# Linear attention beside routed tokens: which of the first transfers ScalarE issues first, and where the router's vector takes its turn

## The chip, the cores and the metric

The kernel runs on one core of one Trainium2 chip. The metric is the device time of one execution in microseconds. The kernel is one program for five engines that run side by side: TensorE (PE, matrix products and transposes; its weight loads are shown apart as PEld), VectorE (DVE), ScalarE (ACT), GpSimd (POOL) and SyncE (SP), which only issues transfers. SyncE and ScalarE each have a queue of transfers between HBM and the on-chip memory; in the profile SyncE's is q1 and ScalarE's is q10. An engine works through its own instructions in program order and waits for others by semaphores.

## The reference

One input x (2048 tokens of 640, bf16) is normalised per token, and two blocks are added to it:

```python
x = A_x
xn = _layernorm(x, axis=-1)
return x + _A_ref(xn, A_wqkv, A_wo) + _B_ref(xn, B_w_r, B_w_gate, B_w_up, B_w_down)
```

`_A_ref` is linear attention with 32 heads of 20: `qkv = xn @ wqkv`; `phi(t) = where(t > 0, t + 1, exp(t)) + 1e-6` on q and k; `kv = pk^T v` and `z = sum of pk` per head; the result is `(pq @ kv) / (pq . z + 1e-6)`, times `wo`.

`_B_ref` scores each token, `r = xn @ w_r`, takes the 8 tokens with the highest score, sends them through a gated layer (`silu(x w_gate) * (x w_up)`, times `w_down`), scales with `sigmoid(r)` and adds them back in their places; all tokens of xn are passed on too.

What matters here: `w_r` is a vector of 640 numbers, used once, for the scores. The k part of `wqkv` is 640 x 640. Both multiply the normalised tokens, so that both need the tokens turned (features on the partitions).

## The kernel before

The 2048 tokens are 16 tiles of 128 (`T = 16`), each with 640 features, which are 5 blocks of 128 (`KC = 5`). The program is one straight list written out by hand; no planner reorders it, so the order of the calls in the source is the order on each engine.

For each tile: its 160 KB of x are loaded by SyncE's queue into `x_sb`; VectorE takes statistics of the two halves (`ln_stats`, lines 165 and 168, then 169); the inverse root of the variance comes from ScalarE for tiles 0 and 1 (`root="A"`, lines 178 and 179, a logarithm and an exponential) and from GpSimd for later ones (lines 171 and 174); VectorE scales (`ln_scale`, line 183) into `xn`. Tiles 0 to 4 are turned by TensorE (`turn_pe`, line 195), and the turned blocks are copied from PSUM to `xnT` (`turned`, lines 203 and 205); later tiles are turned by a transfer. TensorE then makes k (`k_one` and `k_mm`, line 213), ScalarE and VectorE form phi(k) (`k_act`, `k_phi`), and TensorE gathers `xn^T phi(k)` (`g_mm`, line 274). From tile 4 on a loop interleaves k of one tile, a unit of q (`q_mm`, line 247) and the gathering of the tile before. Then come the routing, the small products per head, the eight chosen tokens, and the output loop (`o_mm`, line 789; `o_add`, line 799).

The first part, around the change:

- SyncE issues x tiles 0, 1 and 2 (lines 125, 127, 129), each 160 KB, then tile 3 (line 151) after a small GpSimd instruction. Tiles 4 and up are issued behind a GpSimd copy of tile 0's inverse root (line 303).
- ScalarE issues `wr_rows`, the vector w_r as 5 rows of 128, 1.2 KB (line 126), then the k weights in two pieces: feature blocks 0 to 2, 480 KB (line 128), and 3 to 4, 320 KB (line 130). Then it loads its table of functions.
- TensorE runs filler matmuls on a zeroed tile (`warm`, line 294) until there is work. Between the seventh and the eighth filler it turns w_r's rows into a column for each feature block (line 299) in PSUM bank 2; ScalarE copies them to `wrT` (line 310) ahead of its copy of the turned tile 0.
- `wrT` is used twice: as the last column of the k weights (`wk_sb[:, :, D]`, line 324), so that the scores of tiles 1 and up come with k, and by itself for tile 0 (line 331).
- Tile 0's k has its first six matmuls (feature blocks 0 to 2, lines 320 to 322) ahead of the turn of tile 1, its last four behind it.

Of the kernel before, what the change touches and what calls it, by code (L numbers as in the profile page):

```python
# [8 lines left out]
P = 128  # L9
S = 2048  # L10
D = 640
# [4 lines left out]
KC = D // P  # L16
# [29 lines left out]
def kernel(  # L46
# [13 lines left out]
    nc = tc.nc  # L60
# [4 lines left out]
    wqkv_v = A_wqkv.rearrange("(kc p) n -> p kc n", p=P)  # L65
# [9 lines left out]
    def sb(shape, dt, name, pool=None, tag=None):  # L75
        return (pool or big).tile(shape, dt, tag=tag or name, name=name)
# [6 lines left out]
    wk_sb = sb([P, KC, D + 1], BF16, "wk_sb")  # L83
# [8 lines left out]
    ident = sb([P, P], BF16, "ident")  # L92
# [14 lines left out]
    wr_rows = sb([KC, P], BF16, "wr_rows")  # L107
    wrT = sb([P, KC], BF16, "wrT")
# [10 lines left out]
    def psb(b):  # L119
        return ps[:, b, :].bitcast(BF16)  # L120
# [2 lines left out]


    nc.sync.dma_start(x_sb[:, 0, :], x_v[:, 0, :])
    nc.scalar.dma_start(wr_rows[:], B_w_r.rearrange("(kc p) -> kc p", p=P))
    nc.sync.dma_start(x_sb[:, 1, :], x_v[:, 1, :])
    nc.scalar.dma_start(wk_sb[:, 0:3, 0:D], wqkv_v[:, 0:3, D : 2 * D])
    nc.sync.dma_start(x_sb[:, 2, :], x_v[:, 2, :])
    nc.scalar.dma_start(wk_sb[:, 3:KC, 0:D], wqkv_v[:, 3:KC, D : 2 * D])  # L130
    nc.scalar.preload_act_table_set("natural_log_exp_and_others")
# [27 lines left out]
    def ln_stats(t, parts="abr", root="P"):  # L159
        if "a" in parts:  # L160
            st = lnp.tile([P, 2, nc.vector.BN_STATS_DIM], F32, tag="st", name=f"st{t}")
            mv = lnp.tile([P, 2], F32, tag="mv", name=f"mv{t}")
            rs = lnp.tile([P, 2], F32, tag="rs", name=f"rs{t}")
            stat[t] = (st, mv, rs)
            nc.vector.bn_stats(out=st[:, 0, :], in_=x_sb[:, t, 0:HW])  # L165
        if "b" in parts:
            st, mv, rs = stat[t]
            nc.vector.bn_stats(out=st[:, 1, :], in_=x_sb[:, t, HW:D])  # L168
            nc.vector.bn_aggr(out=mv[:], in_=st[:])  # L169
            if root == "P":  # L170
                nc.gpsimd.tensor_tensor(  # L171
                    out=rs[:, 0:1], in0=mv[:, 1:2], in1=half[:, 0:1], op=ALU.add
                )
                nc.gpsimd.tensor_tensor(  # L174
                    out=rs[:, 1:2], in0=rs[:, 0:1], in1=half[:, 1:2], op=ALU.pow
                )
            else:
                nc.scalar.activation(rs[:, 0:1], mv[:, 1:2], AF.Ln, bias=half[:, 0:1])
                nc.scalar.activation(rs[:, 1:2], rs[:, 0:1], AF.Exp, scale=-0.5)

    def ln_scale(t):
        _, mv, rs = stat.pop(t)
        nc.vector.tensor_scalar(  # L183
            out=xn[:, t, :], in0=x_sb[:, t, :], scalar1=mv[:, 0:1], scalar2=rs[:, 1:2],
            op0=ALU.subtract, op1=ALU.mult,
        )
# [6 lines left out]
    def turn_pe(t, b):  # L193
        for kc in range(KC):
            nc.tensor.transpose(
                psb(b)[:, kc * P : (kc + 1) * P], xn[:, t, kc * P : (kc + 1) * P], ident[:]
            )

    def turned(t, b, eng, c0=0, c1=KC):
        src = psb(b)[:, c0 * P : c1 * P].rearrange("p (k f) -> p k f", f=P)  # L200
        dst = xnT[:, c0:c1, t * P : (t + 1) * P]
        if eng == "A":
            nc.scalar.copy(dst, src)
        else:
            nc.vector.tensor_copy(dst, src)  # L205
# [86 lines left out]
    def warm(n, w=512):  # L292
        for _ in range(n):
            nc.tensor.matmul(
                ps[:, 0, 0:w], lhsT=GT[:, 0, 0:P], rhs=GT[:, 0, 0:w], start=True, stop=True
            )

    warm(N_WARM)
    nc.tensor.transpose(psb(2)[:, 0:KC], wr_rows[:], ident[0:KC, 0:KC])
    warm(1)  # L300
    ln_stats(0, root="A")

# [4 lines left out]
    for t0 in range(8, T, 2):  # L307
        nc.sync.dma_start(x_sb[:, t0 : t0 + 2, :], x_v[:, t0 : t0 + 2, :])
    ln_stats(1, "a")
    nc.scalar.copy(wrT[:], psb(2)[:, 0:KC])  # L310
    warm(6, P)
    ln_scale(0)
    ln_stats(1, "b", root="A")
    turn_pe(0, 7)
    warm(4, P)
    turned(0, 7, "V", 0, 2)
    turned(0, 7, "A", 2, KC)
    ln_scale(1)
    ln_stats(2, "a")
    for kc in range(3):  # L320
# [546 lines left out]
```

## Time and profile before

| | |
|---|---|
| three runs | 110.76, 110.76, 110.89 us; median 110.76 |
| profiled execution | 110.76 us; its span, first to last instruction, 109.0 us |
| TensorE busy | 103.2 us (95% of the span), 873 matmuls |
| VectorE, ScalarE, GpSimd busy | 82.6, 57.8, 30.0 us |
| moved by transfers | 22.59 MB, 207 GB/s over the span |
| granted TensorE clock | 1.000 |

The page gives the busy time of each engine, the chain of waits (followed back from the last instruction to what released each step), and groups of instructions. A busy TensorE isn't a TensorE at its peak: matmuls are pipelined, and their ends are modelled, so the spacing of the starts tells the speed. In the timeline, a row has the start, the length, the engine ("q" behind its name means that it only issues), the line, the operation, output and input, and the count; in brackets stands how long the engine was idle ahead of it and what ended that. The table by stretches has for each stretch its bounds, its length, the busy time and count for each engine, the granted clock, the busy share of the transfer engines and the rate in GB/s. In the view of transfers, a queue's row has the packets, the MB and the share of the 16 transfer engines' time, and an issue's row the KB of each and the time from issue to landing. A wait for several semaphores is put down to the one that came last.

### The profile page before, as it was taken

Reading aid. Unit: us, or ns where it says so; the run is one execution under the profiler, and the core shown is the slowest. Engines: PE = TensorE matmul, PEld = TensorE weight load, DVE = VectorE, ACT = ScalarE, POOL = GpSimd, SP = SyncE. Lnnn points to the kernel's source line nnn. Section 1 sums busy time; section 2 is a strip of 40 time slices with the busy share of each in tenths; the row PEclk is TensorE's granted clock in tenths of the full one; section 3 lists DMA queues with packets and bytes.
Section 4 is the critical chain, followed back from the end, with each engine's and each line's share of the span. In section 5 each row is a group of like instructions: output and inputs, shape, how many; then the busy total and the mean of one; then the engine's idle time right before and its main releaser. Section 6 shows DMA issues by size and latency. Waiting matters only on the chain.

```text
span 109.0 us, 2409 instructions
## 1 busy us (share of the span) xinstructions
PE 103.2 (95%) x873; PEld 65.5 (60%) x881; DVE 82.6 (76%) x182; ACT 57.8 (53%) x121; POOL 30.0 (27%) x86
## 2 busy tenths in 40 slices
PE   4989999999999999999999999999999999999980
PEld 1365565566555655566556588965656577777760
DVE  0787988989888797997698892567786669966670
ACT  1557746855785568655875583876798330000000
POOL 7406033667744987640000002200420000000000
PEclk9999999999999999999999999999999999999999
DMA  3999950263999999999955799425226927983333
GB/s 75 316 317 316 332 211 17 46 123 60 274 225 192 197 359 180 311 372 322 368 184 191 211 280 382 161 68 163 70 20 187 353 70 214 317 317 120 127 122 115
DMA packets 23096, 22.59 MB, mean 207 GB/s; under 512 B 8796, under 2 KB 21804, under 8 KB 23084
## 3 DMA queue, kind: packets, MB, share of 16 engines
q1 hardware_dynamic: 21106, 20.37, 64.6%
q10 hardware_dynamic: 1834, 2.02, 5.3%
q0 software_dynamic: 144, 0.04, 0.6%
q8 instruction: 7, 0.11, 0.4%
q14 instruction: 5, 0.04, 0.2%
HBM read 14.52 MB, written 5.28 MB: 182 GB/s over the span
## 4 chain that ended last, share of the span: by engine, by line
PE 86%; DVE 6%; DMA 3%; issue 1%; ACT 0%; SPq 0%; DVEq 0%
PE ps L247 20%; PE ps L789 19%; PE ps L213 18%; PE ps L274 16%; PE ps L283 4%; DMA x_sb<-in_A_x_dram 3%; PE ps L620 2%; PE ps L672 2%; PE ps L651 2%; DVE xn L799 1%; DVE st L165 1%; PE ps L580 1%; DVE xn L183 1%; PE ps L502 1%; DVE st L168 1%
## 5 line engine op out<-in xcount | busy, mean ns | idle before, releaser
L213 PE MATMUL ps<-wk_sb,xnT 128*128 128x320 bf16 (+1 forms) x160 | 25.0, 300 | 0.5 <-DMA wk_sb<-in_A_wqkv_dram 0.4
L247 PE MATMUL ps<-xnT,wq_sb 128*128 128x512 bf16 x95 | 23.6, 379 | 0.4 <-issue 0.2
L789 PE MATMUL ps<-late,pqT 128*128 128x320 bf16 (+2 forms) x165 | 22.3, 295 | 0.0
L213 PEld LDWEIGHTS <-xnT 128*128 128x128 bf16 x160 | 15.3, 98 | 9.2 <-DVE xnT L205 0.8
L274 PE MATMUL ps<-pk,xn 128*128 128x512 bf16 x77 | 19.3, 379 | 0.3 <-issue 0.2
L229 ACT ACTIVATE ek<-ps 128x640 bf16<-128x640 f32 x16 | 11.3, 705 | 15.6 <-PE ps L213 15.6
L789 PEld LDWEIGHTS <-pqT 128*128 128x128 bf16 x165 | 15.8, 98 | 6.3 <-issue 0.2
L799 DVE TENSOR_TENSOR xn<-ps,x_sb 128x640 bf16<-128x640 f32 (+3 forms) x18 | 13.2, 749 | 5.5 <-PE ps L789 5.5
L247 PEld LDWEIGHTS <-wq_sb 128*128 128x128 bf16 x100 | 11.5, 118 | 7.8
L266 DVE SCALAR_TENSOR_TENSOR pqT<-eq,rq 128x512 bf16<-128x512 bf16 x20 | 13.8, 688 | 2.9 <-ACT rq L260 2.8
L236 DVE SCALAR_TENSOR_TENSOR pk<-ek,rk 128x640 bf16<-128x640 bf16 x16 | 12.8, 803 | 2.0 <-ACT rk L230 2.0
L259 ACT ACTIVATE eq<-ps 128x512 bf16<-128x512 f32 x20 | 12.3, 617 | 2.7 <-PE ps L247 2.7
L274 PEld LDWEIGHTS <-xn 128*128 128x128 bf16 x80 | 7.7, 98 | 8.4
L260 ACT ACTIVATE rq<-ps 128x512 bf16<-128x512 f32 x20 | 12.3, 616 | 0.0
L230 ACT ACTIVATE rk<-ps 128x640 bf16<-128x640 f32 x16 | 11.2, 700 | 0.0
L171 POOL TENSOR_TENSOR rs<-mv,half 128x1 f32<-128x1 f32 x14 | 6.3, 447 | 17.1 <-DVE mv L169 17.0
L174 POOL TENSOR_TENSOR rs<-rs,half 128x1 f32<-128x1 f32 x14 | 10.6, 760 | 1.1
L165 DVE BATCH_NORM_STATS2 st<-x_sb 128x6 f32<-128x320 bf16 x16 | 7.7, 478 | 3.3 <-DMA x_sb<-in_A_x_dram 3.3
L183 DVE TENSOR_SCALAR xn<-x_sb,mv,rs 128x640 bf16<-128x640 bf16 x16 | 7.2, 451 | 3.7 <-POOL rs L174 3.3
L565 POOL COPY xsT<-xnT 128x5 bf16 x8 | 1.6, 205 | 21.9 <-DVE junk L693 18.4
L168 DVE BATCH_NORM_STATS2 st<-x_sb 128x6 f32<-128x320 bf16 x16 | 7.6, 476 | 0.0
L189 DVE TENSOR_TENSOR x_sb<-x_sb,xn 128x640 bf16<-128x640 bf16 x16 | 6.9, 476 | 0.0
(123 smaller groups left out, 92.4 us busy)
## 6 DMA issues: line engine op xcount, KB each, us to landing
x_sb<-in_A_x_dram SPq DMA_DIRECT2D x6, 320.0 KB, 8.4
wg_sb<-in_B_w_gate_dram SPq DMA_DIRECT2D x5, 384.0 KB, 4.2
wu_sb<-in_B_w_up_dram SPq DMA_DIRECT2D x5, 384.0 KB, 5.6
wd_sb<-in_B_w_down_dram SPq DMA_DIRECT2D x3, 640.0 KB, 8.5
xxd<-x_sb SPq DMA_DIRECT2D x2, 640.0 KB
out_dram<-xn SPq DMA_DIRECT2D x8, 160.0 KB, 1.9
x_sb<-xxd SPq DMA_DIRECT2D x2, 640.0 KB, 5.0
out_dram<-xn ACTq DMA_DIRECT2D x7, 160.0 KB, 3.1
```

The source lines that it names most:

```text
L174: nc.gpsimd.tensor_tensor(out=rs[:, 1:2], in0=rs[:, 0:1], in1=half[:, 1:2], op=ALU.pow)
L213: nc.tensor.matmul(ps[:, b + h, 0:w], lhsT=xnT[:, kc, t * P : (t + 1) * P], rhs=wk_sb[:, kc, h * HW : h * HW + w], start=(kc == 0), stop=( ...
L229: nc.scalar.activation(e[:], ps[:, b : b + 2, 0:HW], AF.Exp)
L230: nc.scalar.activation(r[:], ps[:, b : b + 2, 0:HW], AF.Relu)
L236: nc.vector.scalar_tensor_tensor(out=pk[:, t, :].rearrange("p (b f) -> p b f", b=2), in0=e[:], scalar=1.0, in1=r[:], op0=ALU.min, op1=ALU.add,
L247: nc.tensor.matmul(ps[:, b, :], lhsT=wq_sb[:, kc, :].rearrange("p (f m) -> p m f", m=KC)[:, m, :], rhs=xnT[:, kc, tb * TBLK : (tb + 1) * T ...
L259: nc.scalar.activation(e[:], ps[:, b, :], AF.Exp)
L260: nc.scalar.activation(r[:], ps[:, b, :], AF.Relu)
L266: nc.vector.scalar_tensor_tensor(out=pqT[:, m, tb * TBLK : (tb + 1) * TBLK], in0=e[:], scalar=1.0, in1=r[:], op0=ALU.min, op1=ALU.add,)
L274: nc.tensor.matmul(ps[:, c, :], lhsT=xn[:, t, c * P : (c + 1) * P], rhs=pk[:, t, 0:512], start=(t == 0), stop=(t == T - 1),)
L789: nc.tensor.matmul(ps[:, b, 0 : c1 - c0], lhsT=pqT[:, kc, t * P : (t + 1) * P], rhs=M_sb[:, kc, c0:c1], start=(kc == 0), stop=(kc == KC - 1),)
L799: nc.vector.tensor_tensor(out=xn[:, t, c0:c1].rearrange("p (b f) -> p b f", f=w), in0=ps[:, b : b + n, 0:w], in1=x_sb[:, t, c0:c1].rearran ...
```

## The change

ScalarE no longer issues w_r; its first transfer is the first piece of the k weights. SyncE issues w_r, third, between tiles 1 and 2 of x. TensorE turns w_r's rows directly behind the turn of tile 0, ahead of four fillers, instead of between fillers at the start, and ScalarE copies the result behind its copy of the turned tile 0 instead of ahead of it. No computation is added or removed.

```diff
     nc.sync.dma_start(x_sb[:, 0, :], x_v[:, 0, :])
-    nc.scalar.dma_start(wr_rows[:], B_w_r.rearrange("(kc p) -> kc p", p=P))
+    nc.scalar.dma_start(wk_sb[:, 0:3, 0:D], wqkv_v[:, 0:3, D : 2 * D])
     nc.sync.dma_start(x_sb[:, 1, :], x_v[:, 1, :])
-    nc.scalar.dma_start(wk_sb[:, 0:3, 0:D], wqkv_v[:, 0:3, D : 2 * D])
+    nc.sync.dma_start(wr_rows[:], B_w_r.rearrange("(kc p) -> kc p", p=P))
     nc.sync.dma_start(x_sb[:, 2, :], x_v[:, 2, :])
     nc.scalar.dma_start(wk_sb[:, 3:KC, 0:D], wqkv_v[:, 3:KC, D : 2 * D])
     nc.scalar.preload_act_table_set("natural_log_exp_and_others")
...
     warm(N_WARM)
-    nc.tensor.transpose(psb(2)[:, 0:KC], wr_rows[:], ident[0:KC, 0:KC])
     warm(1)
     ln_stats(0, root="A")
...
     ln_stats(1, "a")
-    nc.scalar.copy(wrT[:], psb(2)[:, 0:KC])
     warm(6, P)
     ln_scale(0)
     ln_stats(1, "b", root="A")
     turn_pe(0, 7)
+    nc.tensor.transpose(psb(2)[:, 0:KC], wr_rows[:], ident[0:KC, 0:KC])
     warm(4, P)
     turned(0, 7, "V", 0, 2)
     turned(0, 7, "A", 2, KC)
+    nc.scalar.copy(wrT[:], psb(2)[:, 0:KC])
     ln_scale(1)
```

## The prediction

> **What bounds the kernel now.** I read the first line of the page and its chain of waits, then the chain's opening in order of time.
>
> ```profile
> span 109.0 us, 2409 instructions
> PE 86%; DVE 6%; DMA 3%; issue 1%; ACT 0%; SPq 0%; DVEq 0%
> ...
> 1.25 3.16 DMA x_sb<-in_A_x_dram
> ...
> 9.58 0.47 PE ps L195 x5
> ...
> 10.49 1.56 PE ps L213 x10
> ...
> 87.32 17.23 PE ps L789 x126
> ```
>
> From 10.49 us on, TensorE carries the chain almost alone. What comes before is a lead-in, and it hangs on one transfer: tile 1 of x, issued at 1.25, landed 3.16 later, at 4.41. The profiled execution took 110.76 us, which is also the median of the three runs; 1.76 of it lies around the span. The sum below is made on 110.76. A difference under 0.2% (0.22 us) can't be told from none here.
>
> The timeline of the first 8 us (start, length, engine, line; in brackets the idle time ahead and what ended it) shows the lead-in:
>
> ```profile
> 0.79 0.57 ACTq L126 DMA_DIRECT2D wr_rows<-in_B_w_r_dram  x1
> 0.80 0.40 SPq L125 DMA_DIRECT2D x_sb<-in_A_x_dram  x1
> 1.25 0.42 SPq L127 DMA_DIRECT2D x_sb<-in_A_x_dram  x1
> 1.39 0.42 ACTq L128 DMA_DIRECT2D wk_sb<-in_A_wqkv_dram  x1
> 1.71 0.43 SPq L129 DMA_DIRECT2D x_sb<-in_A_x_dram  x1
> 1.84 0.50 ACTq L130 DMA_DIRECT2D wk_sb<-in_A_wqkv_dram  x1
> ...
> 3.14 0.49 DVE L165 BATCH_NORM_STATS2 st<-x_sb 128x6 f32<-128x320 bf16 x1 [3.14 <-DMA x_sb<-in_A_x_dram]
> ...
> 4.44 0.49 DVE L165 BATCH_NORM_STATS2 st<-x_sb 128x6 f32<-128x320 bf16 x1 [0.16 <-DMA x_sb<-in_A_x_dram]
> ...
> 4.70 0.20 ACT L179 ACTIVATE rs<-rs 128x1 f32<-128x1 f32 x1
> ...
> 4.94 0.45 DVE L183 TENSOR_SCALAR xn<-x_sb,mv,rs 128x640 bf16<-128x640 bf16 x1
> ...
> 5.44 0.45 PE L195 MATMUL ps<-ident,xn 128*128 128x128 bf16 x5
> ...
> 6.47 0.99 PE L213 MATMUL ps<-wk_sb,xnT 128*128 128x320 bf16 x6 [0.36 <-DMA wk_sb<-in_A_wqkv_dram]
> 6.50 0.46 ACT L203 COPY xnT<-ps 128x384 bf16<-128x384 bf16 x1
> ...
> 6.99 0.49 DVE L165 BATCH_NORM_STATS2 st<-x_sb 128x6 f32<-128x320 bf16 x1
> 7.01 0.11 PEld L213 LDWEIGHTS <-xnT 128*128 128x128 bf16 x2 [0.17 <-ACT xnT L203]
> ...
> 7.35 0.21 ACT L324 COPY wk_sb<-wrT 128x5 bf16<-128x5 bf16 x1 [0.39 <-DMA wk_sb<-in_A_wqkv_dram]
> ...
> 7.78 0.75 ACT L203 COPY xnT<-ps 128x256 bf16<-128x256 bf16 x2 [0.21 <-PE ps L195]
> ```
>
> VectorE works in program order: statistics of tile 0 (3.14), the first half of tile 1's (4.44, released by tile 1's landing), then the scaling of tile 0 at 4.94. That scaling needs two things: the half-statistics of tile 1, queued ahead of it, done at 4.93; and the inverse root of tile 0, done on ScalarE at 4.90. So the two first x tiles are balanced to 0.03 us. If x tile 0 is used at A and tile 1 at B, the scaling starts at the later of A + 1.80 (3.14 to 4.94) and B + 0.50 (4.44 to 4.94). Everything up to 10.49 follows from it in a fixed order.
>
> **The change, part by part.**
>
> *The waits it removes.* The first half of the k weights holds TensorE for 0.36 us before 6.47, the second half holds ScalarE for 0.39 before 7.35. Neither sets the end. TensorE's third pair of k matmuls waits anyway for ScalarE's copy of the turned tile (6.50 + 0.46 = 6.96; the load at 7.01). ScalarE's next copy at 7.78 waits for the turn of tile 1. So earlier weights are worth 0, at most the 0.03 above, if tile 1 too came earlier.
>
> *The moved instructions on TensorE and ScalarE.* The w_r turn (below) and its copy change places; the turn goes into TensorE's idle 0.36 ahead of 6.47, the copy into ScalarE's idle 0.39 and 0.21 ahead of 7.35 and 7.78. Behind the turn stand four filler matmuls, then the k matmuls. Without that cover they would cost 0.18 and 0.15; I take 0.
>
> ```profile
> 4.37 0.29 ACT L178 ACTIVATE rs<-mv,half 128x1 f32<-128x1 f32 x1 [0.72 <-DVE mv L169]
> ...
> 4.47 0.18 PE L299 MATMUL ps<-ident,wr_rows 5*128 5x5 bf16 x1
> 4.59 0.80 PE L294 MATMUL ps<-GT 128*128 128x512 bf16 x7
> ...
> 4.81 0.15 ACT L310 COPY wrT<-ps 128x5 bf16<-128x5 bf16 x1
> ```
>
> *The issue queues.* ScalarE loses 0.57 at its front: the k weights are issued at 0.79 and about 1.24 instead of 1.39 and 1.84, and the table load moves up too, worth nothing since ScalarE then idles 0.72 until 4.37. On SyncE w_r's 0.57 goes between tiles 1 and 2 of x: tile 2 is issued at 2.28 instead of 1.71.
>
> *The order of the transfers* is the term that decides. The 480 KB of k weights was issued behind both x0 and x1 (1.39 after 0.80 and 1.25). Now it goes level with x0 and 0.46 ahead of x1. Does a transfer on ScalarE's queue hold up one on SyncE's? Two stretches of the DMA view (packets, MB, share of 16 engines; then issues, KB and time to landing) answer. The first is 4.10 to 4.50 us, followed by the row of x tile 2 (issued 1.71); the second 89.5 to 92.9:
>
> ```profile
> q10 hardware_dynamic: 115, 0.15, 104.8%
> ...
> x_sb<-in_A_x_dram SPq DMA_DIRECT2D x1, 160.0 KB, 4.7
> ```
>
> ```profile
> q1 hardware_dynamic: 530, 0.66, 67.4%
> ...
> x_sb<-xxd SPq DMA_DIRECT2D x2, 640.0 KB, 5.0
> out_dram<-xn ACTq DMA_DIRECT2D x1, 160.0 KB, 4.4
> ```
>
> In the first, only ScalarE's queue (q10, the k weights) moves packets, although tile 2 of x was issued on SyncE's queue (q1) at 1.71 and lands only 4.7 later. In the second, only q1 moves: a store issued on ScalarE's queue in that stretch has not one packet before a 640 KB reload issued ahead of it is through, and lands 4.4 us later. So I read: the engines take transfers in order of issue, over both queues.
>
> Then x1 lands when x0, the k weights' 480 KB and x1 itself, 800 KB or 819 kB, are through; before it took x0 and x1, 328 kB. What moved by when comes from the table by stretches (last column GB/s):
>
> ```profile
> 0.00:2.50 2.50, 1.13 (x3) 0.43 (x4) 0.00 (x0) 0.13 (x1) 1.83 (x11) 1.00 0.26 62
> 2.50:3.50 1.00, 1.00 (x4) 0.32 (x3) 0.36 (x1) 1.00 (x1) 0.86 (x3) 1.00 0.88 190
> 3.50:4.50 1.00, 1.00 (x4) 0.16 (x2) 0.80 (x4) 0.28 (x2) 0.42 (x2) 1.00 1.00 352
> 4.50:5.00 0.50, 0.50 (x5) 0.30 (x5) 0.49 (x2) 0.43 (x3) 0.03 (x1) 1.00 1.07 389
> 5.00:6.00 1.00, 0.95 (x16) 0.72 (x13) 0.96 (x4) 0.00 (x0) 0.15 (x1) 1.00 1.04 379
> ```
>
> Sums: 155 kB by 2.50, 345 by 3.50, 697 by 4.50, 891 by 5.00, 1270 by 6.00. So 819 kB have started at 4.81. From that mark to the use of the data there is a lag (the slowest engine, the landing): x0's 164 kB are reached at 2.55 and used at 3.14, lag 0.59; x1's 328 kB at 3.41, used 4.44, lag 1.03; the first k weights' 819 kB at 4.81, used 6.47, lag 1.66. x1 behind the weights is then used at 5.40, 5.84 or 6.47. I take x1's own lag: 5.84, that is +1.40; ends +0.96 and +2.03.
>
> Who is first of x0 and the weights is close: SyncE's issue of x0 runs 0.80 to 1.20, ScalarE's of the weights would run 0.79 to 1.21. I take x0 first, by the end of the issue; it then keeps 3.14, and x1 decides. The other way round is a rival.
>
> *What is late next.* By the same sums x2, now behind 1.28 MB (6.15 plus its present lag of 1.17, from 983 kB at 5.24 to 6.41), is there at 7.3; its statistics stand at 6.99 + 1.40 = 8.39. w_r (1148 kB, 5.68, lag 0.59 to 1.66) is there between 6.3 and 7.3, and TensorE comes to its turn at 5.44 + 0.45 + 1.40 = 7.29. Nothing further on waits. The later loads of x hang on tile 0's root and move with it.
>
> **Sum**: 110.76 + 1.40 (x1) + 0 (TensorE, ScalarE, issue) = 112.16, about 112.2; by the two ends 111.7 and 112.8.
>
> **The rivals.**
>
> 1. *The weights go ahead of x0.* For it: 0.79 stands before 0.80. Then x0 needs 640 KB (655 kB, started at 4.38), is used at 4.97 to 5.41 by lags of 0.59 and 1.03, and A + 1.80 puts the scaling at 6.77 to 7.21: +1.83 to +2.27, mid 112.8.
>
> 2. *The engines share between the queues.* x0 is then through with as much of the weights, 328 kB (3.41), used at 4.00 to 4.44: A + 1.80 gives 5.80 to 6.24, +0.86 to +1.30; x1, at 656 kB, 4.38 + 1.03 = 5.41, gives +0.97. About +1.0: 111.8. Against it: the two stretches above, in which one queue stood still. The Trainium skill ("DMA: Bandwidth & Descriptors", section "Queues, rings and completion order") states this rule: each engine goes round the queues it has work for. By it the sum would be this rival's; the two stretches disagree.
>
> 3. *Not slower: SyncE's queue goes first.* If the x tiles keep the engines and the weights only fill gaps, x1 stays at 4.44 and nothing on the chain moves: 110.76 less 0 to 0.03, so 110.7. It decides at x1's landing: up to 4.41 no loss, from there each 0.1 costs 0.1. For it: x0 and x1 landed ahead of the weights before. Against: from 4.10 to 4.50 SyncE's tile 2 stood still for ScalarE's weights.
>
> 4. *The clock falls.* With the scaling late by 1.40, TensorE idles from 5.39 (4.59 + 0.80) to 6.84. Its first matmuls are slow, its later ones fast:
>
> ```profile
> 1.37 3.17 PE L294 MATMUL ps<-GT 128*128 128x512 bf16 x7 [1.37 <-POOL GT L134]
> ```
> ```profile
> 77.29 5.78 PE ps L247 x26
> ```
>
> 0.45 us each against 0.22. Were it to fall back for as long as the first warming took (1.37 to 4.54, 3.2 us), the k matmuls up to 10.49 would lose half of that, 1.6: 113.8. For it: no row shows TensorE idle so long at this place. Against: the table by stretches grants 1.00 throughout (though in the slow start too). The Trainium skill ("TensorE: Matmul & The Clock Gate", Part 1) puts the fall at an idle window of about 3.4 us; 1.45 is under it, and no run here shows the limit.
>
> **How the numbers follow.** Forecast (x0, weights, x1): 0.38, its own range 111.7 to 112.8. Weights ahead of x0: 0.25. Sharing: 0.15. SyncE first: 0.10. Clock: 0.08. The 0.04 left: a gain from a place that I don't see, such as x0 coming earlier with w_r out of its way. The range 110.7 to 113.2 takes in the first four but for their tails and leaves the clock out. Slower by over 0.2%: forecast, weights ahead, sharing and clock, 0.86, and a little of the third rival, 0.87. Within 0.2%: the rest of the third, 0.09. Faster: 0.04.
>
> **What would show it.** Right: the statistics of tile 1 (L165, second) start near 5.8 and end a long wait for the transfer of x; the scaling of tile 0 starts 0.5 behind them; no wait for wk_sb on TensorE or ScalarE; the turn of tile 2 near 11.0 and then the old rows, shifted. Weights ahead: the first L165 starts near 5.0 instead of 3.14. Sharing: it starts at 4.0 to 4.4. Wrong: both L165 within 0.1 of 3.14 and 4.44 and the turn of tile 2 still at 9.58; or L213's matmuls twice as far apart as the ten from 10.49 (1.56 in all), the clock.

## The result, and the profile after

Before, 110.81 us (median of six, 110.76 to 110.89); with the change 112.37 us (median of six, 111.63 to 113.17): a ratio of 1.014, 95% interval 1.0114 to 1.0166. Slower, as forecast, and 0.17 from the predicted 112.2. But no execution was there. Three took 111.63, 111.67 and 111.89, three took 112.85, 113.05 and 113.17. The profiled one is the slowest, 113.17 with a span of 111.5. So there are two things to explain: about 0.8 to 1.1 us in every execution, and about 1.3 more in some. In all comparisons the ratio leaves out an execution over 1.5% above the fastest of its kernel; there are two, 112.45 and 113.12 below.

The timeline of the lead-in after (columns as in the prediction):

```profile
0.79 0.47 ACTq L126 DMA_DIRECT2D wk_sb<-in_A_wqkv_dram  x1
...
0.80 0.40 SPq L125 DMA_DIRECT2D x_sb<-in_A_x_dram  x1
...
1.25 0.42 SPq L127 DMA_DIRECT2D x_sb<-in_A_x_dram  x1
...
1.38 4.24 PE L294 MATMUL ps<-GT 128*128 128x512 bf16 x14 [1.38 <-POOL GT L134]
...
3.35 0.49 DVE L165 BATCH_NORM_STATS2 st<-x_sb 128x6 f32<-128x320 bf16 x1 [3.35 <-DMA x_sb<-in_A_x_dram]
...
5.42 0.49 DVE L165 BATCH_NORM_STATS2 st<-x_sb 128x6 f32<-128x320 bf16 x1 [0.94 <-DMA x_sb<-in_A_x_dram]
...
5.83 0.43 DVE L183 TENSOR_SCALAR xn<-x_sb,mv,rs 128x640 bf16<-128x640 bf16 x1
...
6.32 0.71 PE L195 MATMUL ps<-ident,xn 128*128 128x128 bf16 x5 [0.71 <-DVE xn L183]
...
7.48 1.81 PE L213 MATMUL ps<-wk_sb,xnT 128*128 128x320 bf16 x6
...
7.97 0.21 ACT L324 COPY wk_sb<-wrT 128x5 bf16<-128x5 bf16 x1
...
11.96 0.44 PE L195 MATMUL ps<-ident,xn 128*128 128x128 bf16 x5
```

Three things are to be seen. The waits for the k weights are gone (L213 at 7.48 and L324 at 7.97 have none). Tile 1 of x is used at 5.42 instead of 4.44, and VectorE waits 0.94 for it; the scaling of tile 0 starts at 5.83 instead of 4.94, 0.89 later. And TensorE is slow: the six k matmuls take 1.81 where they took 0.99. Tile 2's turn, the hand-over to TensorE's long run, is 2.38 later than at 9.58: 0.89 from tile 1, 1.49 from what TensorE did in between. The executions' times differ by 113.17 - 110.76 = 2.41.

Was it the order of the transfers? The view of transfers after, from 3.05 to 3.95 us (packets, MB, share of the 16 engines):

```profile
q10 hardware_dynamic: 252, 0.32, 103.2%
```

Only ScalarE's queue moves anything, the k weights; tile 1 of x, issued at 1.25 on SyncE's, stands still for 0.9 us. Tile 0, issued at 0.80, 0.01 behind the weights, was not held up like that. The same view from 1.30 to 2.60 us:

```profile
q1 hardware_dynamic: 100, 0.12, 49.0%
q10 hardware_dynamic: 1, 0.00, 2.2%
```

Up to there SyncE's queue moved tile 0 nearly alone.

### The profile page after: what moved, and what is told of

Its sections match the earlier page's. It is cut to its first block, busy times and chain, and to the rows that moved or that the text cites. A ratio compares the mean times of both kernels' runs of the same rounds, so it can differ in the third digit from the quotient of the medians.

```text
span 111.5 us, 2409 instructions
## 1 busy us (share of the span) xinstructions
PE 105.4 (95%) x873; PEld 67.1 (60%) x881; DVE 82.6 (74%) x182; ACT 57.9 (52%) x121; POOL 30.0 (27%) x86
## 4 chain that ended last, share of the span: by engine, by line
PE 89%; DMA 4%; DVE 2%; issue 1%; SPq 0%; DVEq 0%
PE ps L213 21%; PE ps L247 19%; PE ps L789 18%; PE ps L274 15%; PE ps L283 4%; DMA x_sb<-in_A_x_dram 4%; PE ps L195 2%; PE ps L620 2%; PE ps L672 2%; PE ps L651 1%; DVE xn L799 1%; PE ps L580 1%; PE ps L502 1%; PE ps L748 1%; PE ps L294 0%
## 5 line engine op out<-in xcount | busy, mean ns | idle before, releaser
L213 PE MATMUL ps<-wk_sb,xnT 128*128 128x320 bf16 (+1 forms) x160 | 26.4, 311 | 0.2 <-DVE xnT L205 0.2
L213 PEld LDWEIGHTS <-xnT 128*128 128x128 bf16 x160 | 15.9, 101 | 9.1 <-DVE xnT L205 0.5
```

Of the source, the lines that this page charges most:

```text
L213: nc.tensor.matmul(ps[:, b + h, 0:w], lhsT=xnT[:, kc, t * P : (t + 1) * P], rhs=wk_sb[:, kc, h * HW : h * HW + w], start=(kc == 0), stop=( ...
```

## The experiments

Each is a small edit, timed beside the kernel before, which took 110.75 to 110.78 us (medians of 20 to 23) in these comparisons. Two theories were to be told apart for the two groups of times: *order and clock* (tile 1 always behind the weights; TensorE's pace differs by execution) and *a race* (in the upper group the weights also go ahead of tile 0).

### The changed kernel again

> The changed kernel once more, for the spread of its times and a second profile. Theory (order and clock): tile 1 of x always lands behind the first k weights, +0.9 us, and in some executions TensorE, idle while it waits, stays at its slow pace, about +1.4 more: two groups, 111.6 to 111.9 and 112.8 to 113.2. In a profile of the upper group the six k matmuls of tile 0 take 1.8 us, in one of the lower 1.0; the first statistics start at 3.1 to 3.4 in both. Rival (a race for the first place): in the upper group the weights went ahead of tile 0 of x, and the first statistics start at 5.0 or later.

Median 111.53 (111.45 to 112.83, six executions): five at 111.45 to 111.56 and one at 112.83. Ratio 1.0091 (1.0055 to 1.0126). The profile is of the lower group (111.50):

```profile
1.37 4.23 PE L294 MATMUL ps<-GT 128*128 128x512 bf16 x14 [1.37 <-POOL GT L134]
...
3.51 0.49 DVE L165 BATCH_NORM_STATS2 st<-x_sb 128x6 f32<-128x320 bf16 x1 [3.51 <-DMA x_sb<-in_A_x_dram]
...
5.26 0.49 DVE L165 BATCH_NORM_STATS2 st<-x_sb 128x6 f32<-128x320 bf16 x1 [0.62 <-DMA x_sb<-in_A_x_dram]
...
5.67 0.43 DVE L183 TENSOR_SCALAR xn<-x_sb,mv,rs 128x640 bf16<-128x640 bf16 x1
...
6.16 0.45 PE L195 MATMUL ps<-ident,xn 128*128 128x128 bf16 x5 [0.55 <-DVE xn L183]
...
6.99 1.18 PE L213 MATMUL ps<-wk_sb,xnT 128*128 128x320 bf16 x6
...
10.29 0.45 PE L195 MATMUL ps<-ident,xn 128*128 128x128 bf16 x5
```

Tile 0 is in time to within 0.4 in both groups (3.35 and 3.51), and tile 1 is late in both (5.42 and 5.26). The race would have shown tile 0 at 5.0 in the upper group, and it is at 3.35. What differs is the six matmuls: 1.18 here, 1.81 there, and the turn of tile 2, 10.29 here. Here it is 0.71 later than before the change, and the scaling of tile 0 is 0.73 later: in the lower group tile 1's delay passes through whole, and nothing is added.

The 14 fillers took as long here as in the upper group's profile, 113.17 (4.23 and 4.24). Then TensorE idled 0.55 and came back fast (tile 0's turn in 0.45); there it idled 0.71 and came back slow (0.71). The trace also records when the clock was raised, which the views don't show (they print 1.00 ahead of the rise as well): at 4.8 us in the kernel before, at 5.7 here, as the gap begins, and at 10.8 in the upper group's profile. The spacing of the k matmuls' starts agrees: there it goes from 0.27 to 0.14 us at about that time.

### TensorE kept busy

```diff
-    warm(6, P)
+    warm(18, P)
     ln_scale(0)
```

> The changed kernel with 18 fillers of 128 columns instead of 6 ahead of the turn of tile 0, so that TensorE idles under 0.6 us there. Theory (order and clock): the upper group is gone, all runs at 111.6 to 111.9. Rival (race between the two queues): the groups stay, the median up to 113.

> The changed kernel with 18 fillers once more, for the spread. Theory (order and clock): again no run above 112; 111.4 to 111.9. Rival (the upper group doesn't depend on the fillers): one run in three near 113.

Medians 111.64 (111.46 to 111.79, five executions) and 111.70 (111.61 to 111.90, five); ratios 1.0074 (1.0061 to 1.0087) and 1.0081 (1.0068 to 1.0094). None of the ten is in the upper group, against four of twelve without the fillers; the six executions of the run with a third of the weights ahead (below), which has the same fillers, aren't there either. As the order theory wants, the lower group stays. In the second profile (111.90) the fillers kept TensorE from idling although they ran slowly:

```profile
1.37 5.51 PE L294 MATMUL ps<-GT 128*128 128x512 bf16 x26 [1.37 <-POOL GT L134]
...
6.68 0.74 PE L195 MATMUL ps<-ident,xn 128*128 128x128 bf16 x5
```

There the fillers themselves hold up the real work: tile 0's turn starts 0.87 behind the scaling (at 5.81), where it is 0.49 in the two profiles of the change without them.

### A gap for TensorE, transfers as before

```diff
     warm(N_WARM)
     nc.tensor.transpose(psb(2)[:, 0:KC], wr_rows[:], ident[0:KC, 0:KC])
-    warm(1)
...
-    warm(6, P)
     ln_scale(0)
```

> The kernel before, transfers untouched, without the eighth 512-column filler and the six of 128 columns, so that TensorE idles from about 4.6 to 5.4 us, about as long as in the changed kernel. Theory (idle time keeps the slow pace): two groups, one at 110.7 to 111.0 and one 1.0 to 1.6 higher, in which tile 0's six k matmuls take 1.6 to 1.8 us. Rival (the upper group comes from the transfers alone): all runs at 110.7 to 111.0.

Median 111.92 (ratio 1.0075, 1.004 to 1.011): two executions at 110.72 and 110.75, seven from 111.83 to 112.45. This is the kernel before with fewer fillers, and the upper group is there without any change in the transfers. The profile (112.35):

```profile
5.48 0.71 PE L195 MATMUL ps<-ident,xn 128*128 128x128 bf16 x5 [0.82 <-DVE xn L183]
...
6.58 1.78 PE L213 MATMUL ps<-wk_sb,xnT 128*128 128x320 bf16 x6
...
11.19 0.44 PE L195 MATMUL ps<-ident,xn 128*128 128x128 bf16 x5
```

An idle 0.82 us, the six matmuls at 1.78, the turn of tile 2 at 11.19 instead of 9.58: 1.6 later. The clock was raised at 10.3. TensorE's idle time in the lead-in is enough for the upper group; the rival that the transfers alone make it has fallen. With the fillers' result this is shown from both sides, though the twelve and ten executions of the changed kernel are few.

### All first transfers on one queue, tile 1 ahead

```diff
     nc.sync.dma_start(x_sb[:, 0, :], x_v[:, 0, :])
-    nc.scalar.dma_start(wk_sb[:, 0:3, 0:D], wqkv_v[:, 0:3, D : 2 * D])
     nc.sync.dma_start(x_sb[:, 1, :], x_v[:, 1, :])
+    nc.sync.dma_start(wk_sb[:, 0:3, 0:D], wqkv_v[:, 0:3, D : 2 * D])
     nc.sync.dma_start(wr_rows[:], B_w_r.rearrange("(kc p) -> kc p", p=P))
     nc.sync.dma_start(x_sb[:, 2, :], x_v[:, 2, :])
-    nc.scalar.dma_start(wk_sb[:, 3:KC, 0:D], wqkv_v[:, 3:KC, D : 2 * D])
+    nc.sync.dma_start(wk_sb[:, 3:KC, 0:D], wqkv_v[:, 3:KC, D : 2 * D])
```

> The changed kernel with all first transfers on SyncE's queue in the order x0, x1, first k weights, w_r, x2, last k weights; the turn of w_r stays where the change put it. Theory (order): tile 1 is used at 4.4 to 4.5 again, and the time is 110.8, within 0.15. Rival (what costs is w_r's late turn, its copy or its place ahead of x2): 111.5 or more, with tile 1 at 4.4.

Median 111.07 (eleven of twelve from 110.57 to 111.36, one at 113.12, for which no cause is shown); ratio 1.0019 (1.0004 to 1.0034). More than expected. The profile (111.33), and two rows of its chain of waits:

```profile
4.14 0.44 DVE L165 BATCH_NORM_STATS2 st<-x_sb 128x6 f32<-128x320 bf16 x1
...
4.89 0.45 DVE L183 TENSOR_SCALAR xn<-x_sb,mv,rs 128x640 bf16<-128x640 bf16 x1 [0.31 <-ACT rs L179]
...
7.28 0.49 DVE L165 BATCH_NORM_STATS2 st<-x_sb 128x6 f32<-128x320 bf16 x1 [0.25 <-DMA x_sb<-in_A_x_dram]
...
8.64 0.49 DVE L165 BATCH_NORM_STATS2 st<-x_sb 128x6 f32<-128x320 bf16 x1 [0.22 <-DMA x_sb<-in_A_x_dram]
...
10.13 0.45 PE L195 MATMUL ps<-ident,xn 128*128 128x128 bf16 x5
```
```profile
1.71 5.11 DMA wk_sb<-in_A_wqkv_dram
...
6.87 1.11 PE ps L213 x6
```

Tile 1 no longer waits at all, and tile 0's root (0.31) now sets the scaling of tile 0. The order theory is right there. But what stands behind tile 1 on the one queue comes later. The first k weights, issued at 1.71 instead of 1.39, land at 6.82, and the first k matmul runs at 6.87 instead of 6.47; tiles 2 and 3 come late too, with waits of 0.25 and 0.22. Tile 2's turn is 0.55 later than before, as much as this execution is over 110.78. The chain goes through the weights and then through TensorE alone, whose clock was raised only at 7.1; VectorE's scaling of tile 2 ends only about 0.05 sooner, so that both paths are late together. The rival named w_r, which isn't in the chain.

### The change with the weights held back 0.6 us

```diff
+    nc.gpsimd.memset(GT[:, 0, 0:512], 0.0)
+    nc.gpsimd.memset(wk_sb[:, 0, 0:2], 0.0)
     nc.scalar.dma_start(wk_sb[:, 0:3, 0:D], wqkv_v[:, 0:3, D : 2 * D])
...
-    nc.gpsimd.memset(GT[:, 0, 0:512], 0.0)
     make_identity(nc, ident[:])
```

> The changed kernel with the first k weights held until a small GpSimd write at about 1.35 us, so that they are issued at about 1.4 as before the change; w_r stays third on SyncE's queue, its turn behind tile 0's. Theory (order): tile 1 is used at 4.2 to 4.5, the time is 110.8, within 0.2. Rival (w_r ahead of x2, or its late turn, costs): 111.2 or more with tile 1 at 4.4.

Median 110.88 (110.77 to 111.74), ratio 1.0023 (1.0007 to 1.0039); seven of twelve at 110.77 to 110.92. Everything else of the change is there: w_r on SyncE's queue, its late turn, its late copy. The profile (110.77; its line numbers are one higher):

```profile
4.18 0.44 DVE L166 BATCH_NORM_STATS2 st<-x_sb 128x6 f32<-128x320 bf16 x1
...
4.92 0.45 DVE L184 TENSOR_SCALAR xn<-x_sb,mv,rs 128x640 bf16<-128x640 bf16 x1 [0.30 <-ACT rs L180]
...
6.26 1.18 PE L214 MATMUL ps<-wk_sb,xnT 128*128 128x320 bf16 x6
...
7.15 0.21 ACT L325 COPY wk_sb<-wrT 128x5 bf16<-128x5 bf16 x1
...
9.56 0.45 PE L196 MATMUL ps<-ident,xn 128*128 128x128 bf16 x5
```

So 0.6 us in the issue of ScalarE's transfers decides the first part of the loss. And this run settles what the removed waits were worth: here too L214 and L325 wait for no weights, the first k matmul runs at 6.26 instead of 6.47, and the turn of tile 2 is at 9.56 instead of 9.58: 0.02. The five executions from 111.01 to 111.74 weren't expected. TensorE's pace is the likely cause (the next run shows such a case), but the profile is of another execution, so that stays open.

### The turn of w_r alone

The kernel before with L299 and L310 moved as in the change, transfers untouched.

> The kernel before with only w_r's turn on TensorE and its copy on ScalarE moved as in the change; the transfers as before. Theory (order): 110.8, within 0.15; turn and copy go into idle time. Rival (the moved turn costs, or takes warming away): above 111.0.

Median 110.79 (110.66 to 111.03, ten), ratio 0.9998 (0.9989 to 1.0007). The moved turn and copy cost nothing that these executions show. The profiled one is the highest, and its chain of waits begins with slow fillers:

```profile
1.38 4.23 PE ps L294 x14
5.61 0.55 PE ps L195 x5
```

Tile 0 is scaled at 4.94 as before, and TensorE has no gap, but its clock was raised only at 7.2 (before: 4.8), and tile 2's turn starts at 9.78 instead of 9.58. So a late rise costs a little even without a gap.

### A third of the weights ahead

```diff
-    nc.scalar.dma_start(wk_sb[:, 0:3, 0:D], wqkv_v[:, 0:3, D : 2 * D])
+    nc.scalar.dma_start(wk_sb[:, 0:1, 0:D], wqkv_v[:, 0:1, D : 2 * D])
...
-    nc.scalar.dma_start(wk_sb[:, 3:KC, 0:D], wqkv_v[:, 3:KC, D : 2 * D])
+    nc.scalar.dma_start(wk_sb[:, 1:KC, 0:D], wqkv_v[:, 1:KC, D : 2 * D])
...
-    warm(6, P)
+    warm(18, P)
```

> The changed kernel with the 18 fillers, ScalarE's first piece of the k weights cut to one block (160 KB), the other four (640 KB) second. Theory (order, cost by bytes ahead): a third of the bytes stand ahead of tile 1, which is used near 4.5 instead of 5.3 to 5.5, and tile 0's root then decides: 110.9 to 111.3. The second piece is issued level with tile 1 and could still hold it; then 111.5. Rival (any transfer of weights ahead costs the same): 111.6.

Median 111.48 (111.28 to 111.86), ratio 1.0066 (1.0049 to 1.0083): the case that the expectation named second. Its timeline, and the view of transfers from 3.05 to 3.95 us:

```profile
1.22 0.46 ACTq L130 DMA_DIRECT2D wk_sb<-in_A_wqkv_dram  x1
...
1.25 0.44 SPq L127 DMA_DIRECT2D x_sb<-in_A_x_dram  x1
...
3.90 0.49 DVE L165 BATCH_NORM_STATS2 st<-x_sb 128x6 f32<-128x320 bf16 x1 [3.90 <-DMA x_sb<-in_A_x_dram]
...
5.29 0.49 DVE L165 BATCH_NORM_STATS2 st<-x_sb 128x6 f32<-128x320 bf16 x1 [0.26 <-DMA x_sb<-in_A_x_dram]
```
```profile
q10 hardware_dynamic: 189, 0.23, 75.5%
q1 hardware_dynamic: 88, 0.09, 29.2%
```

Here both queues move at once. Each x tile was issued within 0.03 us of a piece of weights (0.80 against 0.79; 1.25 against 1.22), and each was slowed: tile 0 is used at 3.90, tile 1 at 5.29. As a dose it failed: the second piece, issued sooner because the first was smaller, caught tile 1, and tile 0 at 3.90 would by itself put the scaling where it is, at 5.70 (3.90 + 1.80). That the cost goes by the bytes ahead was not shown by it. Nor does a close issue alone decide: in the changed kernel tile 0 was as close to the weights and went nearly alone up to 2.60 us. The ends of the issues (start plus length) would fit both (there 1.20 against 1.26 for the weights, here 1.20 against 1.19), but two cases don't show a rule.

### What the early tile 1 could be used for

With tile 1 in time, VectorE waits 0.30 for tile 0's root. Two kernels put tile 1's second half of statistics into that wait: the gated one, and the kernel before (edit the same).

```diff
     ln_stats(1, "a")
+    nc.vector.bn_stats(out=stat[1][0][:, 1, :], in_=x_sb[:, 1, HW:D])
...
-    ln_stats(1, "b", root="A")
+    ln_stats(1, "bh", root="A")
```

("h" leaves out the second half there.)

> The gated kernel (weights held to 1.4 us), and tile 1's second half of statistics ahead of the scaling of tile 0 on VectorE, in the 0.3 us in which VectorE waits for tile 0's root. Theory (tile 0's root bounds once tile 1 is early): tile 1's statistics are free, its root comes 0.3 to 0.4 us sooner, the turn of tile 2 starts at 9.2 to 9.4 instead of 9.56: 110.4 to 110.6, some runs higher where TensorE's idle keeps it slow. Rival (x2, x3 or TensorE bound next): 110.8.

> The kernel before with the same move on VectorE. Theory: it gains only as far as tile 1 lands early: with tile 1 used at 4.44 the scaling of tile 0 would start at 5.26 instead of 4.94 and the gain of 0.4 behind it leaves 0.1; with tile 1 at 3.9 the gain is 0.3 to 0.4. 110.4 to 110.8. Rival (nothing gained): 110.8.

The gated one: 110.81 (110.55 to 111.42), ratio 1.0011 (0.9995 to 1.0027), short of the 110.4 to 110.6 that was expected. The kernel before: 110.63 (110.32 to 111.01), ratio 0.9989 (0.9978 to 1.0001). In the second's profile (110.32) the step does what it should:

```profile
4.54 0.47 DVE L311 BATCH_NORM_STATS2 st<-x_sb 128x6 f32<-128x320 bf16 x1
...
4.93 0.44 DVE L184 TENSOR_SCALAR xn<-x_sb,mv,rs 128x640 bf16<-128x640 bf16 x1
...
6.13 0.44 DVE L184 TENSOR_SCALAR xn<-x_sb,mv,rs 128x640 bf16<-128x640 bf16 x1
...
9.17 0.44 PE L196 MATMUL ps<-ident,xn 128*128 128x128 bf16 x5
```

The scaling of tile 1 moves from 6.63 to 6.13, the turn of tile 2 from 9.58 to 9.17, and that execution is 0.45 under the median before. Over twelve executions the gain is 0.1 and its interval reaches no change: it isn't a proven better version. The gated one's profile (110.59) shows what bounds next, from its chain of waits:

```profile
1.37 4.23 PE ps L296 x14
5.61 0.42 PE ps L197 x5
```

Here the chain is TensorE's from its first filler on, whose clock was raised at 5.8; tile 2's turn starts at 9.38. That is the TensorE bound of the rival. What the executions up to 111.42 lost is not shown.

## Why the prediction was right, and where it was not

**What bounds the kernel: right, with one size off.** The lead-in hung on the first two x tiles. I took tile 1's path as B + 0.50 and called the two balanced to 0.03. After, it is 5.42 to 5.83, 0.41: VectorE starts the next instruction before the last one's row ends. So tile 1 had 0.09 to spare before, and tile 0's root, not tile 1, set the scaling: in the profile of the turn alone tile 1 is used at 4.20 and tile 0 is scaled at 4.94 all the same.

**The order of the transfers: right in kind, too large.** The 480 KB of weights, issued 0.46 ahead, were served ahead of tile 1 over both queues, and tile 0 ahead of them, as I had taken it by the end of its issue. I took tile 1's use at 5.84; it came at 5.42 (5.26 to 5.51 in the four profiles of this order, two of them with fillers), near the lower end that I gave, 5.40. Both parts, when the bytes start and the lag behind that, were too large. The table by stretches after:

```profile
0.00:2.50 2.50, 1.12 (x3) 0.44 (x4) 0.00 (x0) 0.67 (x1) 1.82 (x11) 1.00 0.26 47
2.50:3.50 1.00, 1.00 (x4) 0.32 (x3) 0.14 (x1) 0.61 (x1) 0.86 (x3) 1.00 0.88 270
3.50:4.50 1.00, 1.00 (x4) 0.44 (x3) 0.95 (x3) 0.00 (x0) 0.43 (x2) 1.00 1.05 387
4.50:5.00 0.50, 0.50 (x5) 0.23 (x3) 0.00 (x0) 0.39 (x2) 0.00 (x0) 1.00 1.08 382
...
7.00:8.00 1.00, 1.00 (x8) 0.77 (x8) 0.79 (x3) 0.94 (x5) 0.00 (x0) 1.00 0.93 309
```

118 kB by 2.50, 388 by 3.50, 775 by 4.50, so 819 kB at 4.62 (I had 4.81), and a lag of 0.80 (I had 1.03). So the term is +0.98 at the landing and, less the 0.09 to spare, +0.89 at the scaling; in the lower group's profile +0.73. I had +1.40.

**The sum came out near the median by luck, from two errors.** One term was too large by 0.5 to 0.7; another, TensorE's pace, I had left out, and it adds 1.3 in some executions (112.83 against 111.50 in one comparison) and 0 in the others. The six happened to split three and three, so that their median fell in the empty space between the groups. In the second series of six it was 111.53.

**The rivals.** *The clock* had 0.08, a price of 1.6 and stood outside the range; it should have been part of the forecast. Its price was near: 1.3 to 1.4 between the means of the two groups, in both series of the changed kernel and with the gap. Its mechanism was put wrongly: TensorE didn't fall back after the idle time. In the upper group's profile all 14 fillers up to 5.6 us are slow already (1.38 + 4.24; before, the seven from 4.59 took 0.80), and the fast pace comes later still. So the idle time *delays the first rise*: in the ten profiles in which no gap of over 0.15 us came ahead of the rise, it came at 4.8 to 7.3 us, and in the two in which the gap (0.71 and 0.82) came first, at 10.8 and 10.3. My argument against was the granted clock of the table by stretches, and it says nothing here: the stretch from 7.00 to 8.00 above has 1.00 while the k matmuls run at half speed. The Trainium skill ("TensorE: Matmul & The Clock Gate", Part 1) has the rise after a busy window of about 3.4 us that runs free of the kernel's start. The traces agree that the earliest rise stands 3.4 us behind the first filler (4.8 against 1.37). Two groups by where that window falls would fit it, and the gap and filler runs agree; that the window's phase is the cause is argued, not shown. I had applied only the page's rule for the fall.

*Weights ahead of tile 0* (0.25) fell: tile 0 was used at 3.35 to 3.70 in the four profiles of the changed order, not at 5. Yet it lost 0.2 to 0.6, which I had at 0; why stays open. *Sharing* (0.15) came nearer with its numbers (tile 1 at 5.41, 111.8) to the lower group than my forecast did, but not with its mechanism: its sign, tile 0 used at 4.0 to 4.4, isn't there, and tile 1 had no packet for 0.9 us. In the run with a third of the weights ahead both queues moved at once. *SyncE first* (0.10) fell.

**What I costed at nothing** held: w_r's turn and copy (ratio 0.9998 alone), the removed waits (0.02 with them gone and tile 1 in time), x2 and w_r behind the weights (no wait for x2 after; w_r's turn at 6.96, directly behind tile 0's).

## What to carry to other kernels

A wait off the path to the end is no reason to move its transfer up: ask first what the transfer will then stand ahead of, over all queues, because the engines that move data may serve them in one line. Before trusting a sum to a tenth, look at the single executions; a median between two groups describes neither. And filler work that keeps TensorE busy until its first real work isn't free to lose: a transfer that comes 0.9 us later can open an idle gap that costs more than the delay. More fillers aren't free either: while they run slowly they can hold up the real work.

## What the runs showed of the hardware

- With 480 KB issued on ScalarE's queue 0.46 us ahead of 160 KB on SyncE's, the second had no packet for 0.9 us while 252 of the first moved. With an issue 0.01 us apart, SyncE's 160 KB went ahead of the 480 KB (100 packets against 1 up to 2.60 us). With a first piece of 160 KB, issued within 0.03 us, both moved at once (189 and 88 packets). The Trainium skill ("DMA: Bandwidth & Descriptors", section "Queues, rings and completion order") states that each engine goes round the queues it has work for; only the last case looks like that, and the view, a sum over 16 engines, doesn't show whether one engine alternates.
- An idle time of 0.7 to 0.8 us on TensorE in the first 7 us put off its fast pace in some executions, at a price of 1.3 to 1.4 us: the clock was raised at 10.3 and 10.8 us, against 4.8 to 7.3 in the profiles without a gap ahead of the rise. The granted clock in the views stayed at 1.00 all the while.
- With the transfers as before, tile 1 of x was used at 4.44 behind a wait of 0.16 (before), but at 4.20 and 4.23 without one in the profiles of the turn alone and of the gap: its landing varies by more than the 0.09 it has to spare.
